# A query's V in one load of 64 keys a partition, between the two loads of the next query's K

## The chip, the cores and the metric

The kernel runs on one core of one Trainium2 chip. The metric is the device time of one execution in microseconds, as the median of several runs; profiles come from one execution each. TensorE (PE) multiplies matrices, VectorE (DVE) and ScalarE (ACT) work elementwise, GpSimd (POOL) does little here, and SyncE (SP) issues nearly all loads; 16 DMA engines move the data.

## The reference

One decode step of a transformer block in float32, for two sequences of one token each: layer norm, attention over a cache of 8192 keys with 16 heads of 256, output projection, residual; then layer norm and a bilinear gated feed-forward layer, residual.

```python
B, Sq, D = 2, 1, 448
H, Sk, Dh = 16, 8192, 256
q = (x @ wq).reshape(B, Sq, H, Dh)            # then heads ahead of tokens
scores = jnp.einsum("bhqd,bhkd->bhqk", q, k_cache) * (Dh ** -0.5)
p = _softmax(scores, axis=-1)
o = jnp.einsum("bhqk,bhkd->bhqd", p, v_cache)
# h = x + attention(layernorm(x)) @ wo
# h2 = h + ((layernorm(h) @ w_gate) * (layernorm(h) @ w_up)) @ w_down
```

The two caches hold 2 x 16 x 8192 x 256 floats each, 268 MB; all other inputs together are some 25 MB.

## The kernel before

A pair of a head and a sequence is called a query; there are 32, and each has its own 8 MiB of K and 8 MiB of V. The keys lie on the 128 partitions, 64 to a partition. A cache load brings half a query's K or V: 4096 keys that follow each other in memory, 32 a partition, so that every partition gets one run of 32 KB. The tile goes into a ring of four slots of 32 KB a partition, which K and V share.

The main loop (lines 306 to 343) runs over n from 0 to 32. Iteration n issues on SP the loads of query n's K and of query n-1's V, by turns: K's first half, V's first half, K's second half, V's second half. After the first V comes, in some iterations, a load of output weights (`load_wo`, 448 KB, where n % 4 is 1 or 3) or of query weights (`load_wq`, 896 KB, where n % 4 is 2). A load waits on SP until its slot of the ring was read for the last time, and whatever follows on SP waits behind it.

DVE scores query n's K: per 16 keys of a partition a product (L239) and a reduction (L242), four such pairs a query, and a maximum at the end (`top`, L249). A slot of K is free after its second product. In between, after the first pair of query n, DVE, PE and ACT make the softmax of query n-1 (`softmax`), and PE then mixes its V with the weights (`mix`, L278): 32 matmuls a query of two keys a partition each, which appear as 64 instructions, 32 for each half of V. `mixed` brings the result into the output projection. Where n % 4 is 3, save in the last such iteration, PE computes the next two heads' queries (`queries`, L212 and L217) between the two halves of a mix; that is in 7 iterations. PE, DVE and ACT work in the order of the code.

In the end come the feed-forward weights: `wg_t` and `wu_t` (3136 KB each) and `wd_t` (3136 KB in three loads) go into the ring as well. PE computes g (L379, `g_ps`), then u (`u_ps`), DVE multiplies the two, and L438 is the last projection. The last V half comes in parts of 16, 8 and 8 keys (`LAST`), the first K half in two of 16 (`FIRST`).

Of the kernel before, what the change touches and what calls it, by code (L numbers as in the profile page):

```python
# [8 lines left out]
F32 = mybir.dt.float32  # L9
# [4 lines left out]
B, D, H, SK, DH, F = 2, 448, 16, 8192, 256, 1792  # L14
EPS = 1e-5
P = 128
# [3 lines left out]
JC = 32  # L20
NCH = SK // (P * JC)
NJ = SK // P

FIRST, LAST = (16, 16), (16, 8, 8)
RING = 4
WQ, WO = 3 * 2 * DH + DH, 2 * D

FG = (512, 512, 384, 384)
# [1 line left out]
NF = F // P  # L30
# [13 lines left out]
def tile_decode_block(  # L44
# [20 lines left out]
    nc = tc.nc  # L65
    ctx.enter_context(tc.manual_schedule())
    const = ctx.enter_context(tc.tile_pool(name="const", bufs=1))
    ring = ctx.enter_context(tc.tile_pool(name="ring", bufs=RING))
    wpool = ctx.enter_context(tc.tile_pool(name="wpool", bufs=2))
# [77 lines left out]
    def load_wq(hp):  # L147
        t = wpool.tile([P, WQ], F32, tag="wq", name=f"wq_{hp}")
        nc.sync.dma_start(t, wq[hp])
        return t  # L150
# [6 lines left out]
            wo_t[h // 2] = wpool.tile([P, 2, WO], F32, tag="wo", name=f"wo_{h // 2}")  # L157
        nc.sync.dma_start(wo_t[h // 2][:, h % 2, :], wo[h])

    def load_cache(src, b, h, c, name, parts=(JC,)):  # L160
        t = ring.tile([P, JC, DH], F32, tag="ring", name=f"{name}_{h}_{b}_{c}")
        n = P * JC
        keys = src[b, h, c * n : (c + 1) * n].rearrange("(p j) d -> p j d", p=P)
        at = 0
        for k in parts:
            nc.sync.dma_start(t[:, at : at + k, :], keys[:, at : at + k, :])
            at += k
        return t

    w_now = load_wq(0)  # L170

# [55 lines left out]
    NQ = H * B  # L227
# [41 lines left out]
        rl_t[i] = work.tile([P, 1], F32, tag="rl", name=f"rl_{i}")  # L269
        nc.vector.reciprocal(rl_t[i], l_t[i])  # L270

    def mix(i, vt, c):

        o, p = o_ps[i % 2], p_t[i]
        for t in range(c * JC // 2, (c + 1) * JC // 2):
            j = 2 * t - c * JC
            g = 32 * (t % 4)
            nc.tensor.matmul(  # L278
                o[g : g + 2, :], p[:, 2 * t : 2 * t + 2], vt[c][:, j : j + 2, :],
                start=(t < 4), stop=(t >= NJ // 2 - 4),  # L280
            )

    def mixed(i):
# [14 lines left out]
        if b == B - 1:  # L298
            w = wo_t[h // 2][:, h % 2, :]
            for c in range(2):  # L300
# [2 lines left out]
                    start=(h == 0 and c == 0), stop=(h == H - 1 and c == 1),  # L303
                )

    for n in range(NQ + 1):
        kt, vt = [], []
        hp, at = divmod(n, 2 * B)
        for c in range(NCH):
            if n < NQ:  # L310
                parts = FIRST if n == 0 and c == 0 else (JC,)
                kt.append(load_cache(k_cache, n % B, n // B, c, "k", parts))
            if n > 0:
                parts = LAST if n == NQ and c == NCH - 1 else (JC,)
                vt.append(load_cache(v_cache, (n - 1) % B, (n - 1) // B, c, "v", parts))
            if c == 0 and at == 1:
                load_wo(2 * hp)
            if c == 0 and at == 3 and hp + 1 < H // 2:
                load_wo(2 * hp + 1)
            if c == 0 and at == 2 and hp + 1 < H // 2:  # L320
                w_t[hp + 1] = load_wq(hp + 1)
        if n == NQ:
            load_wo(H - 1)
        if n < NQ:
            scores(n, kt, 0)
        if n > 0:
            softmax(n - 1)
        if n < NQ:
            scores(n, kt, 1)
        if n > 0:  # L330
            norm(n - 1)
        if n < NQ:
            for part in range(2, 2 * NCH):
                scores(n, kt, part)
        for c in range(NCH):
            if c > 0 and at == 3 and hp + 1 < H // 2:
                q_t[hp + 1] = queries(hp + 1, w_t[hp + 1])
            if n > 0:
                mix(n - 1, vt, c)
        if n > 0:  # L340
            mixed(n - 1)
        if n < NQ:
            top(n)
# [7 lines left out]
    wg_t = load_ff(wg, "wg_t")  # L351
    wu_t = load_ff(wu, "wu_t")

    wd_t = ring.tile([P, NF, D], F32, tag="ring", name="wd_t")
    at = 0
    for n in (8, 4, 2):
        nc.sync.dma_start(
# [145 lines left out]
```

## Time and profile before

| | |
|---|---|
| median of 3 runs | 1314.98 us (1314.97 to 1315.05) |
| the profiled execution | 1314.9 us |
| its span in the trace | 1313.1 us |
| busy: DVE, PE, ACT | 1153.3, 569.9, 60.7 us |
| moved by DMA | 561.64 MB, mean 428 GB/s |

The span is the time in which instructions and transfers are recorded; the execution is 1.8 us longer. Busy times are sums over the span and say nothing yet of what waits for what; the chain that ended last does, and so do the bracketed parts of timeline rows, which give an instruction's idle time before it and what ended that.

### The profile page before, as it was taken

How to read it: one execution, taken by the hardware profiler on the slowest of the kernel's cores; microseconds unless marked ns; L12 is line 12 of the kernel's file. 1: busy time of each engine (PE TensorE's matmuls, PEld its weight loads, DVE VectorE, ACT ScalarE, POOL GpSimd, SP SyncE). 2: the span in 40 equal slices, each digit the busy share in tenths (PEclk: the TensorE clock that was granted, in tenths of full speed). 3: DMA queues.
4: the chain of work that ended last, by engine and by line, in shares of the span. 5: the costliest groups of instructions: out<-in, count | busy, mean ns of one | idle time of the engine just before them, and what ended most of it. 6: DMA issues, size and time to landing. Idle time of an engine off the chain costs nothing.

```text
span 1313.1 us, 6974 instructions
## 1 busy us (share of the span) xinstructions
PE 569.9 (43%) x2936; PEld 173.4 (13%) x2936; DVE 1153.3 (88%) x395; ACT 60.7 (5%) x183; POOL 1.2 (0%) x8
## 2 busy tenths in 40 slices
PE   3224553354432743426433453524525246254357
PEld 2011110111010210102110021101101002011013
DVE  7999999898998899888998889988998989989971
ACT  1000000000000000000000000000000000000000
POOL 0000000000000000000000000000000000000000
PEclk8556766657765666657666567666676667565668
DMA  9999999999999999999999999999999999999997
GB/s 408 430 430 433 430 432 429 428 433 433 431 428 434 430 431 426 435 429 432 431 431 431 434 429 431 430 425 434 430 431 431 433 428 435 431 430 431 431 424 336
DMA packets 23091, 561.64 MB, mean 428 GB/s; under 512 B 2578, under 2 KB 2580, under 8 KB 5908
## 3 DMA queue, kind: packets, MB, share of 16 engines
q1 hardware_dynamic: 23048, 561.20, 99.6%
q8 instruction: 23, 0.38, 0.1%
q14 instruction: 8, 0.07, 0.0%
q10 hardware_dynamic: 12, 0.01, 0.0%
HBM read 561.19 MB, written 0.00 MB: 427 GB/s over the span
## 4 chain that ended last, share of the span: by engine, by line
DMA 79%; PE 14%; DVE 5%; issue 1%; ACT 0%; POOLq 0%; SPq 0%; POOL 0%
DMA v<-in_A_v_cache_dram 77%; PE o_ps L278 13%; DVE prod L239 3%; DMA wu_t<-in_B_w_up_dram 2%; DVE s L242 2%; PE q_ps L199 0%; PE u_ps L379 0%; PE y_ps L438 0%; DVE o_ps L101 0%; PE hm_ps L431 0%; PE oT_ps L291 0%; ACT o_sb L287 0%; PE mean_x L120 0%; DVE xb L134 0%; PE var_x L178 0%
## 5 line engine op out<-in xcount | busy, mean ns | idle before, releaser
L239 DVE TENSOR_TENSOR prod<-k,q 128x4096 f32<-128x4096 f32 x128 | 565.7, 4420 | 115.6 <-DMA k<-in_A_k_cache_dram 110.7
L242 DVE TENSOR_REDUCE s<-prod 128x16 f32<-128x4096 f32 x128 | 565.8, 4420 | 6.0
L278 PE MATMUL o_ps<-v,p 128*2 128x512 f32 x2048 | 371.3, 891 | 338.1 <-DMA v<-in_A_v_cache_dram 338.1
L278 PEld LDWEIGHTS o_ps<-v,p 128*2 128x2 f32 x2048 | 59.2, 109 | 613.6 <-DMA v<-in_A_v_cache_dram 367.3
L257 PE MATMUL nb_ps<-nm,row 1*128 1x1 f32 x64 | 17.9, 347 | 280.0 <-DVE nm L255 280.0
L257 PEld LDWEIGHTS nb_ps<-nm,row 1*128 1x128 f32 x64 | 15.7, 303 | 287.2 <-issue 158.7
L287 ACT ACTIVATE o_sb<-o_ps 128x512 f32<-128x512 f32 x32 | 19.1, 597 | 679.2 <-PE o_ps L278 679.2
L301 PE MATMUL acc_ps<-wo,oT 128*2 128x448 f32 x64 | 43.9, 834 | 5.6 <-ACT oT L297 5.6
L291 PE MATMUL oT_ps<-sel,o_sb 128*128 128x1 f32 x256 | 33.7, 253 | 23.2 <-ACT o_sb L287 23.2
L212 PE MATMUL q_ps<-wq,xb 128*128 128x512 f32 x84 | 39.1, 601 | 0.0
L291 PEld LDWEIGHTS oT_ps<-sel,o_sb 128*128 128x128 f32 x256 | 31.0, 191 | 55.9 <-ACT o_sb L287 55.9
L251 PE MATMUL mT<-ident,m 128*1 128x128 f32 x32 | 10.2, 318 | 61.2 <-DVE m L249 60.9
L266 PE MATMUL l_ps<-lsum,ones 128*128 128x1 f32 x64 | 18.7, 362 | 23.5 <-ACT p L262 23.5
L259 ACT ACTIVATE nb<-nb_ps 128x1 f32<-128x1 f32 x32 | 5.5, 171 | 406.8 <-PE nb_ps L257 406.8
L266 PEld LDWEIGHTS l_ps<-lsum,ones 128*128 128x128 f32 x64 | 16.0, 310 | 26.2 <-ACT p L262 26.2
L212 PEld LDWEIGHTS q_ps<-wq,xb 128*128 128x128 f32 x84 | 15.4, 190 | 20.6 <-issue 20.3
L217 PE MATMUL q_ps<-wq,xb 128*128 128x256 f32 x56 | 14.4, 379 | 0.0
L251 PEld LDWEIGHTS mT<-ident,m 128*1 128x1 f32 x32 | 2.5, 79 | 84.7 <-issue 50.0
L389 DVE TENSOR_TENSOR h_sb<-x_sb,acc_ps 2x448 f32<-2x448 f32 x1 | 0.6, 609 | 13.8 <-PE acc_ps L301 13.8
L222 ACT ACTIVATE q<-q_ps 128x512 f32<-128x512 f32 x14 | 8.4, 597 | 92.1 <-PE q_ps L217 92.1
L217 PEld LDWEIGHTS q_ps<-wq,xb 128*128 128x128 f32 x56 | 10.6, 190 | 7.4 <-issue 6.7
L262 ACT ACTIVATE p<-s,nb 128x64 f32<-128x64 f32 x32 | 11.1, 348 | 1.0
(79 smaller groups left out, 101.8 us busy)
## 6 DMA issues: line engine op xcount, KB each, us to landing
k<-in_A_k_cache_dram SPq DMA_DIRECT2D x63, 4096.0 KB, 26.5
v<-in_A_v_cache_dram SPq DMA_DIRECT2D x63, 4096.0 KB, 33.2
wq<-in_wq_dram SPq DMA_DIRECT2D x8, 896.0 KB, 34.6
wo<-in_wo_dram SPq DMA_DIRECT2D x16, 448.0 KB, 33.5
k<-in_A_k_cache_dram SPq DMA_DIRECT2D x2, 2048.0 KB, 13.5
wg_t<-in_B_w_gate_dram SPq DMA_DIRECT2D x1, 3136.0 KB, 24.5
wu_t<-in_B_w_up_dram SPq DMA_DIRECT2D x1, 3136.0 KB, 30.4
v<-in_A_v_cache_dram SPq DMA_DIRECT2D x1, 2048.0 KB
```

The lines of the kernel that those rows point to most:

```text
L212: nc.tensor.matmul(ps, xb[:, c, b, :], w[:, c * 2 * DH : (c + 1) * 2 * DH], start=(c == 0), stop=False,)
L217: nc.tensor.matmul(ps[:, k * DH : (k + 1) * DH], xb[:, DC - 1 + k, b, :], w[:, 3 * 2 * DH : WQ], start=False, stop=(k == 1),)
L239: nc.vector.tensor_mul(prod, kt[c][:, k * HC : (k + 1) * HC, :], q[:, None, :].to_broadcast([P, HC, DH]))
L242: nc.vector.tensor_reduce(s_t[i][:, part * HC : (part + 1) * HC], prod, axis=AX.X, op=ALU.add)
L251: nc.tensor.transpose(mT_t[i], m, ident)
L257: nc.tensor.matmul(nb_ps, row, nm, start=True, stop=True)
L262: nc.scalar.activation(p_t[i], s_t[i], AF.Exp, bias=nb, scale=DH**-0.5, accum_out=lsum)
L266: nc.tensor.matmul(l_t[i], ones, lsum, start=True, stop=True)
L278: nc.tensor.matmul(o[g : g + 2, :], p[:, 2 * t : 2 * t + 2], vt[c][:, j : j + 2, :], start=(t < 4), stop=(t >= NJ // 2 - 4),)
L287: nc.scalar.activation(o_sb, o_ps[i % 2], AF.Copy)
L291: nc.tensor.matmul(oT_ps[:, c : c + 1], o_sb[:, (2 * k + c) * P : (2 * k + c + 1) * P], sel[:, k : k + 1], start=(k == 0), stop=(k == 1),)
L301: nc.tensor.matmul(acc_ps, oT_t[h][:, c, :], w[:, c * D : (c + 1) * D], start=(h == 0 and c == 0), stop=(h == H - 1 and c == 1),)
```

## The change

V of a query becomes one load of 64 keys a partition, one run of 64 KB in each, into a buffer of its own, `v_sb`, which takes 64 KB a partition; the ring keeps two slots, for K alone. K is loaded in two halves still, but a partition's 64 keys now follow each other in memory, so a half is 32 KB out of every 64. V of query n-1 is loaded between the two halves of query n's K. The first two queries' V come as 16 and 48 keys (`EARLY`), the first of these ahead of the K of the same iteration; for the second query it is issued after the first half of query 0's mix. The last query's V comes as 32, 16, 8 and 8 keys. `wd_t` moves from the ring into `v_sb`. Scores, softmax and mixing keep their instructions; only the keys' order over partitions differs, for K and V alike.

```diff
--- before.py
+++ after.py
@@ -21,8 +21,10 @@
 NCH = SK // (P * JC)
 NJ = SK // P
 
-FIRST, LAST = (16, 16), (16, 8, 8)
-RING = 4
+FIRST = (16, 16)
+
+EARLY, LAST = (16, 48), (32, 16, 8, 8)
+RING = 2
 WQ, WO = 3 * 2 * DH + DH, 2 * D
 
 FG = (512, 512, 384, 384)
@@ -157,15 +159,20 @@
             wo_t[h // 2] = wpool.tile([P, 2, WO], F32, tag="wo", name=f"wo_{h // 2}")
         nc.sync.dma_start(wo_t[h // 2][:, h % 2, :], wo[h])
 
-    def load_cache(src, b, h, c, name, parts=(JC,)):
-        t = ring.tile([P, JC, DH], F32, tag="ring", name=f"{name}_{h}_{b}_{c}")
-        n = P * JC
-        keys = src[b, h, c * n : (c + 1) * n].rearrange("(p j) d -> p j d", p=P)
+    def load_k(b, h, c, parts=(JC,)):
+        t = ring.tile([P, JC, DH], F32, tag="ring", name=f"k_{h}_{b}_{c}")
+        keys = k_cache[b, h].rearrange("(p j) d -> p j d", p=P)
         at = 0
         for k in parts:
-            nc.sync.dma_start(t[:, at : at + k, :], keys[:, at : at + k, :])
+            nc.sync.dma_start(t[:, at : at + k, :], keys[:, c * JC + at : c * JC + at + k, :])
             at += k
         return t
+
+    v_sb = const.tile([P, NJ, DH], F32, name="v_sb")
+
+    def load_v(b, h, at, to):
+        keys = v_cache[b, h].rearrange("(p j) d -> p j d", p=P)
+        nc.sync.dma_start(v_sb[:, at:to, :], keys[:, at:to, :])
 
     w_now = load_wq(0)
 
@@ -269,14 +276,13 @@
         rl_t[i] = work.tile([P, 1], F32, tag="rl", name=f"rl_{i}")
         nc.vector.reciprocal(rl_t[i], l_t[i])
 
-    def mix(i, vt, c):
+    def mix(i, c):
 
         o, p = o_ps[i % 2], p_t[i]
         for t in range(c * JC // 2, (c + 1) * JC // 2):
-            j = 2 * t - c * JC
             g = 32 * (t % 4)
             nc.tensor.matmul(
-                o[g : g + 2, :], p[:, 2 * t : 2 * t + 2], vt[c][:, j : j + 2, :],
+                o[g : g + 2, :], p[:, 2 * t : 2 * t + 2], v_sb[:, 2 * t : 2 * t + 2, :],
                 start=(t < 4), stop=(t >= NJ // 2 - 4),
             )
 
@@ -303,16 +309,26 @@
                     start=(h == 0 and c == 0), stop=(h == H - 1 and c == 1),
                 )
 
+    def loads_v(n):
+
+        parts = EARLY if n <= 2 else LAST if n == NQ else (NJ,)
+        return [((n - 1) % B, (n - 1) // B, sum(parts[:k]), sum(parts[: k + 1])) for k in range(len(parts))]
+
     for n in range(NQ + 1):
-        kt, vt = [], []
+        kt = []
         hp, at = divmod(n, 2 * B)
+        todo = loads_v(n) if n > 0 else []
+        if n == 1:
+
+            load_v(*todo.pop(0))
+        if n == 2:
+            todo.pop(0)
         for c in range(NCH):
             if n < NQ:
-                parts = FIRST if n == 0 and c == 0 else (JC,)
-                kt.append(load_cache(k_cache, n % B, n // B, c, "k", parts))
-            if n > 0:
-                parts = LAST if n == NQ and c == NCH - 1 else (JC,)
-                vt.append(load_cache(v_cache, (n - 1) % B, (n - 1) // B, c, "v", parts))
+                kt.append(load_k(n % B, n // B, c, FIRST if n == 0 and c == 0 else (JC,)))
+            if c == 0:
+                for v in todo:
+                    load_v(*v)
             if c == 0 and at == 1:
                 load_wo(2 * hp)
             if c == 0 and at == 3 and hp + 1 < H // 2:
@@ -336,7 +352,9 @@
             if c > 0 and at == 3 and hp + 1 < H // 2:
                 q_t[hp + 1] = queries(hp + 1, w_t[hp + 1])
             if n > 0:
-                mix(n - 1, vt, c)
+                mix(n - 1, c)
+                if n == 1 and c == 0:
+                    load_v(*loads_v(2)[0])
         if n > 0:
             mixed(n - 1)
         if n < NQ:
@@ -351,7 +369,7 @@
     wg_t = load_ff(wg, "wg_t")
     wu_t = load_ff(wu, "wu_t")
 
-    wd_t = ring.tile([P, NF, D], F32, tag="ring", name="wd_t")
+    wd_t = v_sb.rearrange("p j d -> p (j d)")[:, : NF * D].rearrange("p (n d) -> p n d", d=D)
     at = 0
     for n in (8, 4, 2):
         nc.sync.dma_start(
```

SP's queue in mid-kernel, before: a k or v row is half a query's K or V, named by sequence, half and a running number (`k_1_0_666`: sequence 1, first half); `wq` and `wo` are weights; at the end of a row stand partitions x floats.

```order
L166 DMA k_0_1_594<-in_A_k_cache_dram 128x8192
L166 DMA v_1_1_596<-in_A_v_cache_dram 128x8192
L166 DMA k_1_0_666<-in_A_k_cache_dram 128x8192
L166 DMA v_0_0_668<-in_A_v_cache_dram 128x8192
L158 DMA wo_515<-in_wo_dram 128x896
L166 DMA k_1_1_671<-in_A_k_cache_dram 128x8192
L166 DMA v_0_1_673<-in_A_v_cache_dram 128x8192
L166 DMA k_0_0_758<-in_A_k_cache_dram 128x8192
L166 DMA v_1_0_760<-in_A_v_cache_dram 128x8192
```

K and V take turns here, half by half. The same place after:

```order
L167 DMA k_0_1_581<-in_A_k_cache_dram 128x8192
L167 DMA k_1_0_651<-in_A_k_cache_dram 128x8192
L175 DMA v_sb<-in_A_v_cache_dram 128x16384
L160 DMA wo_505<-in_wo_dram 128x896
L167 DMA k_1_1_655<-in_A_k_cache_dram 128x8192
L167 DMA k_0_0_740<-in_A_k_cache_dram 128x8192
L175 DMA v_sb<-in_A_v_cache_dram 128x16384
L167 DMA k_0_1_743<-in_A_k_cache_dram 128x8192
```

V's two rows of 8192 floats a partition became one of 16384, and the two halves of K around a query's change now follow each other.

SP's queue at the end, before, from the last query's K to the feed-forward weights:

```order
L166 DMA k_1_0_2602<-in_A_k_cache_dram 128x8192
L166 DMA v_0_0_2604<-in_A_v_cache_dram 128x8192
L166 DMA k_1_1_2606<-in_A_k_cache_dram 128x8192
L166 DMA v_0_1_2608<-in_A_v_cache_dram 128x8192
L166 DMA v_1_0_2677<-in_A_v_cache_dram 128x8192
L166 DMA v_1_1_2679<-in_A_v_cache_dram 128x4096
L166 DMA v_1_1_2679<-in_A_v_cache_dram 128x2048 x2
L158 DMA wo_2453<-in_wo_dram 128x896
L348 DMA wg_t<-in_B_w_gate_dram 128x6272
L348 DMA wu_t<-in_B_w_up_dram 128x6272
```

The last K's second half has half a query's V between it and the first. And after:

```order
L167 DMA k_1_0_2515<-in_A_k_cache_dram 128x8192
L175 DMA v_sb<-in_A_v_cache_dram 128x16384
L167 DMA k_1_1_2518<-in_A_k_cache_dram 128x8192
L175 DMA v_sb<-in_A_v_cache_dram 128x8192
L175 DMA v_sb<-in_A_v_cache_dram 128x4096
L175 DMA v_sb<-in_A_v_cache_dram 128x2048 x2
L160 DMA wo_2371<-in_wo_dram 128x896
L366 DMA wg_t<-in_B_w_gate_dram 128x6272
L366 DMA wu_t<-in_B_w_up_dram 128x6272
L375 DMA v_sb<-in_wd_dram 128x3584
```

The second half of the last K now stands behind the whole V of the query before it, and the last V, in four parts, behind that.

## Rows read from the trace of the kernel before

**Rows 1.** The page, parts 1 and 3: busy per engine; queue, packets, MB, share

```profile
PE 569.9 (43%) x2936; PEld 173.4 (13%) x2936; DVE 1153.3 (88%) x395; ACT 60.7 (5%) x183; POOL 1.2 (0%) x8
...
q1 hardware_dynamic: 23048, 561.20, 99.6%
```

**Rows 2.** The page, part 4: the chain that ended last, by engine

```profile
DMA 79%; PE 14%; DVE 5%; issue 1%; ACT 0%; POOLq 0%; SPq 0%; POOL 0%
```

**Rows 3.** Timeline, DVE, 557 to 639: start us, us, engine, line, op, out<-in, idle before

```profile
557.05 4.42 DVE L239 TENSOR_TENSOR prod<-k,q 128x4096 f32<-128x4096 f32 x1 [2.74 <-DMA k<-in_A_k_cache_dram]
...
578.74 4.42 DVE L239 TENSOR_TENSOR prod<-k,q 128x4096 f32<-128x4096 f32 x1 [3.69 <-DMA k<-in_A_k_cache_dram]
...
598.10 4.43 DVE L239 TENSOR_TENSOR prod<-k,q 128x4096 f32<-128x4096 f32 x1 [1.32 <-DMA k<-in_A_k_cache_dram]
...
618.72 4.43 DVE L239 TENSOR_TENSOR prod<-k,q 128x4096 f32<-128x4096 f32 x1 [2.63 <-DMA k<-in_A_k_cache_dram]
...
636.55 0.22 DVE L249 TENSOR_REDUCE m<-s 128x1 f32<-128x64 f32 x1
...
638.15 4.42 DVE L239 TENSOR_TENSOR prod<-k,q 128x4096 f32<-128x4096 f32 x1 [1.38 <-DMA k<-in_A_k_cache_dram]
```

**Rows 4.** Timeline, PE: two places in mid-kernel, then the first query's mix

```profile
609.12 6.02 PE L278 MATMUL o_ps<-v,p 128*2 128x512 f32 x32
...
615.07 2.84 PE L212 MATMUL q_ps<-wq,xb 128*128 128x512 f32 x6
...
621.18 1.03 PE L217 MATMUL q_ps<-wq,xb 128*128 128x256 f32 x4
...
649.16 6.47 PE L278 MATMUL o_ps<-v,p 128*2 128x512 f32 x32
...
58.24 4.99 PE L278 MATMUL o_ps<-v,p 128*2 128x512 f32 x32
...
64.86 3.62 PE L278 MATMUL o_ps<-v,p 128*2 128x512 f32 x32 [1.64 <-DMA v<-in_A_v_cache_dram]
```

**Rows 5.** Timeline, SP's queue: a K load is issued

```profile
611.59 0.33 SPq L166 DMA_DIRECT2D k<-in_A_k_cache_dram  x1
```

**Rows 6.** Timeline, the start: x's load, its first use, the fifth cache load

```profile
0.74 0.55 ACTq L78 DMA_DIRECT2D x_sb<-in_A_x_dram  x1
...
2.26 0.45 PE L141 MATMUL T_ps_x<-ident,x_sb 2*128 2x2 f32 x3 [2.26 <-DMA x_sb<-in_A_x_dram]
...
24.87 0.33 SPq L166 DMA_DIRECT2D k<-in_A_k_cache_dram  x1
```

**Rows 7.** The page, part 2: GB/s in 40 equal slices of 32.8 us

```profile
GB/s 408 430 430 433 430 432 429 428 433 433 431 428 434 430 431 426 435 429 432 431 431 431 434 429 431 430 425 434 430 431 431 433 428 435 431 430 431 431 424 336
```

**Rows 8.** Timeline, the end, 1256 to 1307: DVE, PE and ACT

```profile
1256.39 4.42 DVE L239 TENSOR_TENSOR prod<-k,q 128x4096 f32<-128x4096 f32 x1 [1.50 <-DMA k<-in_A_k_cache_dram]
...
1274.22 0.22 DVE L249 TENSOR_REDUCE m<-s 128x1 f32<-128x64 f32 x1
...
1276.83 7.54 PE L278 MATMUL o_ps<-v,p 128*2 128x512 f32 x56
...
1285.73 1.04 PE L278 MATMUL o_ps<-v,p 128*2 128x512 f32 x8 [1.36 <-DMA v<-in_A_v_cache_dram]
...
1294.40 1.92 PE L379 MATMUL g_ps<-wg_t,xr 128*32 128x512 f32 x8 [0.68 <-DMA wg_t<-in_B_w_gate_dram]
...
1301.25 0.69 ACT L416 ACTIVATE g_sb<-g_ps,rv 128x512 f32<-128x512 f32 x1 [12.41 <-PE g_ps L379]
...
1301.77 3.65 PE L379 MATMUL u_ps<-wu_t,xr 128*32 128x256 f32 x64 [0.60 <-DMA wu_t<-in_B_w_up_dram]
...
1306.75 3.12 PE L438 MATMUL y_ps<-wd_t,hmT 128*2 128x112 f32 x112
```

## The prediction

> **What bounds the kernel now.** I read the page's first part and its queue table, then the chain, then the stretches of DVE, PE and SP around one query, then the last 60 us. [rows 1]: the one busy queue fills the 16 DMA engines for 99.6% of the span; DVE is next with 88%, 1153.3 us, that is 36.0 us for each of the 32 queries. [rows 2]: 79% of the chain is DMA, and what is left is mostly PE. [rows 3]: DVE starts each K tile just when it lands; from 598.10 to 638.15 a query takes 40.05 us, so DVE has about 4 us to spare and PE much more. So in the body only two things count: how fast bytes move, and whether the queue ever runs dry. At the end a chain of compute follows the last loads, and there order counts.
>
> **What the change does to bytes and loads.** Every byte is still loaded once. SP issues 29 cache loads fewer (161 rows become 132): the V of queries 2 to 30 is one load in place of two; the others keep their count. Price of a load: in [rows 3] V and K, 8192 KB, take 638.15 - 618.72 = 19.43 us. With a wo load (448 KB) between them they take 618.72 - 598.10 = 20.62, with a wq load (896 KB) 578.74 - 557.05 = 21.69. At the rate of the 19.43 the two would cost 1.06 and 2.13; they cost 1.19 and 2.26. Both exceed by 0.13 us, whatever their size: about the fixed price of a load of 128 runs. If a 64 KB run costs as much overhead as a 32 KB one, the change saves 29 x 0.13 = 3.8 us; if the gain of longer runs is nothing and a load itself is free, 0. No row shows a 64 KB run, or parts the load's price from that of its runs, so I take the middle, -2 us, and keep 0 and -4. The Trainium skill, "DMA: Bandwidth & Descriptors", section "Where 436 GB/s comes from", puts a ceiling of 435.2 GB/s on the engines' ports; the trace agrees that little is left, with 8192 KB in 19.43 us, 431.7 GB/s. By that page even perfect runs would save an estimated 0.16 us of each V's 19.43, 4.5 us in 29.
>
> K is now read as 32 KB out of every 64 KB. Its runs keep their length and number: 0, unless the pitch matters (a rival).
>
> **Whether the queue runs dry in the body.** Let A be the time when K's second half of query n lands and DVE starts on it. DVE takes 17.83 us to its last reduction (618.72 to 636.55, [rows 3]) and some 18 in all, so it starts K's first half of n+1 at A+18.0; that landed at A+9.7. Landings then follow at 9.72 us a 4096 KB: V(n) at A+29.15, K's second half of n+1 at A+40.05 where a wo lies between, K's first half of n+2 at A+49.8.
> - The slot of K. The ring has two slots; a slot comes free at the second product, 611.59 - 598.10 = 13.5 us after DVE began ([rows 3, 5]). So K's first half of n+2 can be issued at A+31.5 and must be on its way by about A+38.5: a tiny load takes 1.5 us from issue to use (0.74 to 2.26, [rows 6]). 7 us to spare, cost 0. K's second half has more.
> - The V buffer. V(n+1) waits on SP until PE has mixed the whole of V(n), and behind it on SP stand a wo or wq and K's second half of n+2, which DVE awaits. The weights of query n are ready 609.12 - 598.10 = 11.0 us after DVE began on the next K ([rows 3, 4]), at A+29.0, so mixing starts with V's landing, A+29.15. It is 64 instructions. Cold, 32 take 6.0 to 6.5 us; when PE has just been at work, 3.62 ([rows 4]). So a mix takes about 9.7 us and ends at A+38.9. V(n+1) must be issued by A+49.8 - 1.5 = A+48.3. Spare: 9 us.
> - In every fourth iteration, but not the last, 7 in all, the queries of the next head pair stand on PE between the two halves of a mix: 615.07 to 622.21, 7.1 us ([rows 4]). Then the mix ends at A+46.0: still 2 us to spare, cost 0. This is the cover that is thin. If both halves run at 6.47, it ends at A+49.2 and the queue stands still for 1.0 us, seven times.
> - The start. The second query's first 16 keys of V wait for the first mix, which starts at 58.24 and takes 4.99 for a half ([rows 4]), so they go out between 61 and 63.3. Ahead of them stand 26.5 MB, which at the 408 and 430 GB/s of the first slices ([rows 7]) last to 63.4. K's first half of query 1 goes out at 24.87, when DVE frees the first slot ([rows 6]: there it was the fifth cache load), with 11.4 MB ahead of it, to 28. Cost 0, at worst 1.4.
>
> **The end, where the change costs.** Before, the order is K0(31), V0(30), K1(31), V1(30), V0(31), V1(31) in three parts. Now the whole V(30) stands ahead of K1(31). That puts K1(31) 4096 KB later, half of 19.43: it lands not at 1256.39 but at 1266.11 ([rows 8]). All that DVE and PE do with it follows:
> - last reduction of DVE after 1274.22 - 1256.39 = 17.83: 1283.94;
> - first instruction of the last mix after 1276.83 - 1274.22 = 2.61: 1286.55.
> The last part of V(31) has the same bytes ahead of it as before, so it lands when it did, 1285.73, and no longer decides. Before, 56 of the 64 instructions were done while the last parts of V were under way, and 1.04 us was left after the landing: end at 1286.77. Now all 64 come after the softmax: PE has been idle before, so 6.0 + 3.62 = 9.7 us, end at 1296.25, 9.5 us later. Bounds: 7.2 warm (end 1293.8, +7.0) and 12.9 all cold (1299.5, +12.7).
> What hides of this: before, the first down-stream projection started at 1294.40 as its weights landed and ended at 1301.2, and the next one then waited 0.60 us for the wu load ([rows 8]). That 0.6 is absorbed. So u starts at 1301.2 + 9.5 = 1310.7 in place of 1301.77: **+8.9 us**, bounds +6.4 and +12.1. After u nothing waits for a load: wd's 3136 KB follow wu and land by about 1309, while their user, at 1306.75 before ([rows 8]), would start near 1315.7. wd now goes into the V buffer and waits for the first 13 matmuls of the last mix, about 1290, when wg is still moving: 0.
>
> **Sum.** The profiled execution took 1314.9 us (span 1313.1 and 1.8 around it), 0.1 below the median. 1314.9 + 8.9 - 2.0 + 0 = **1321.8**. Its own range: 1314.9 + 6.4 - 4 = 1317.3 to 1314.9 + 12.1 = 1327.
>
> **Rivals.**
> 1. The V buffer stalls the queue: the seven query iterations at cold pace, 7 x 1.0 = 7 us, 1328.8. For it: the 2 us of spare rest on PE running fast after its first half, and the mix at 649.16 stayed at 6.47 through all of its 32 ([rows 4]). Against: the 3.62 and the queries' 7.1 behind a mix of 6.02 show PE fast when it works on. It decides from a mix with queries longer than 19.1 us. 12%.
> 2. The pitch slows the reads: V and K now step 64 KB from partition to partition. If they moved at the pace of the body's slowest slices, 425 GB/s in place of 431 ([rows 7]), the 64 pairs of loads of 19.43 us would grow by 1.4%, 17 us: 1339. Against: wu with its 24.5 KB runs lands 1301.77 - 1294.40 = 7.4 us after wg ([rows 8]), 3136 KB at some 435 GB/s, hardly other than the 32 KB runs, so the step shows no hold so far. 8%. The Trainium skill, "DMA: Bandwidth & Descriptors", section "Latency and other measured facts", tells of lower rates at large power-of-two row pitches, from 512 KiB up; it gives no figure for 64 KB, and no run here shows one.
> 3. Long runs pay for the end: not slower. The engines would have to save 0.3 us of each V's 19.43 to cover the 8.9, twice the 0.13 that the rows bear out, and 0.4 us to be faster: 64 KB runs at 440 GB/s: 29 x 0.4 = 11.6 us, 1312. Only if a run itself costs much more than the excess of wo and wq shows. 12%, half of it faster.
>
> **How the numbers follow.** Forecast 68%, rivals 12, 8 and 12. A change of 0.2%, 2.6 us, is about the least that a measurement of this kernel tells from none. The forecast's low end touches the upper edge of that band (1317.6), 3% of the cases. So faster 0.06, same 0.09, slower 0.85. Range: from the forecast's low end 1317 to 1329, which takes in rival 1 and leaves out rivals 2 and 3, 20%.
>
> **What would show it.** In the profile after: DVE's last K tile starts near 1264 to 1266; the last mix is one block of 64 instructions that starts some 2.6 us after DVE's last reduction and not after a landing; u starts after g and not after wu's landing; the chain's last 50 us are DVE and PE. The DMA share stays at 99% in every slice of the body; one V and two halves of K take about 38.7 us. The prediction is wrong if DVE waits for K longer than some 4 to 6 us in any query (rival 1), if GB/s fall evenly (rival 2) or rise above 435 (rival 3).

## The result

The changed kernel takes 1320.59 us (median of 6 runs, 1318.19 to 1322.65), the kernel before 1314.97 (1314.78 to 1315.05): a ratio of 1.0040, 95% interval 1.0029 to 1.0051. Forecast were 1321.8 us in a range of 1317 to 1329, that is 1.0052, and slower. The profiled execution took 1322.65 us with a span of 1320.8; it is the slowest of the six. New is the scatter: 4.5 us between runs, where the kernel before has 0.3 in this comparison and 1.0 to 2.4, with more runs, in those of the experiments below.

A version found on the way (`e9_best`, below) takes 1313.17 us, 0.9984 of the kernel before (0.9976 to 0.9993).

### The profile page after: what moved, and what is told of

The parts are those of the page before. It is cut to its first block, busy times and chain, and to the rows that moved or that the text cites. A ratio compares the mean times of both kernels' runs of the same rounds, so it can differ in the third digit from the quotient of the medians.

```text
span 1320.8 us, 6916 instructions
## 1 busy us (share of the span) xinstructions
PE 494.1 (37%) x2936; PEld 167.7 (13%) x2936; DVE 1150.8 (87%) x395; ACT 60.7 (5%) x183; POOL 1.2 (0%) x8
## 3 DMA queue, kind: packets, MB, share of 16 engines
q1 hardware_dynamic: 18872, 561.19, 98.9%
## 4 chain that ended last, share of the span: by engine, by line
DMA 62%; DVE 34%; PE 3%; issue 0%; ACT 0%; DVEq 0%; POOLq 0%; POOL 0%
DMA k<-in_A_k_cache_dram 62%; DVE prod L246 22%; DVE s L249 12%; PE o_ps L284 1%; PE g_ps L397 0%; PE q_ps L206 0%; PE u_ps L397 0%; PE y_ps L456 0%; PE acc_ps L307 0%; PE oT_ps L297 0%; DVE o_ps L103 0%; PE hm_ps L449 0%; DVEq L246 0%; DVE h_sb L407 0%; ACT o_sb L293 0%
## 5 line engine op out<-in xcount | busy, mean ns | idle before, releaser
L284 PE MATMUL o_ps<-v_sb,p 128*2 128x512 f32 x2048 | 301.2, 751 | 0.6 <-DMA v_sb<-in_A_v_cache_dram 0.4
L284 PEld LDWEIGHTS o_ps<-v_sb,p 128*2 128x2 f32 x2048 | 54.2, 98 | 214.2 <-issue 211.9
L307 PE MATMUL acc_ps<-wo,oT 128*2 128x448 f32 x64 | 36.2, 701 | 5.6 <-ACT oT L303 5.6
L293 ACT ACTIVATE o_sb<-o_ps 128x512 f32<-128x512 f32 x32 | 19.1, 597 | 271.7 <-PE o_ps L284 271.7
## 6 DMA issues: line engine op xcount, KB each, us to landing
k<-in_A_k_cache_dram SPq DMA_DIRECT2D x63, 4096.0 KB, 19.7
```

The costliest lines, as they stand in the source:

```text
L284: nc.tensor.matmul(o[g : g + 2, :], p[:, 2 * t : 2 * t + 2], v_sb[:, 2 * t : 2 * t + 2, :], start=(t < 4), stop=(t >= NJ // 2 - 4),)
L293: nc.scalar.activation(o_sb, o_ps[i % 2], AF.Copy)
L307: nc.tensor.matmul(acc_ps, oT_t[h][:, c, :], w[:, c * D : (c + 1) * D], start=(h == 0 and c == 0), stop=(h == H - 1 and c == 1),)
```

## The profile after

The page of the changed kernel, parts 1 to 4: busy time, GB/s in 40 slices, the queue, and the chain that ended last. They answer to [rows 1], [rows 7] and [rows 2].

```profile
PE 494.1 (37%) x2936; PEld 167.7 (13%) x2936; DVE 1150.8 (87%) x395; ACT 60.7 (5%) x183; POOL 1.2 (0%) x8
...
GB/s 404 415 439 432 431 437 425 431 431 438 433 429 425 431 431 437 429 427 430 435 432 431 435 425 427 428 448 425 427 422 433 428 442 429 437 421 433 433 422 243
...
q1 hardware_dynamic: 18872, 561.19, 98.9%
...
DMA 62%; DVE 34%; PE 3%; issue 0%; ACT 0%; DVEq 0%; POOLq 0%; POOL 0%
```

DVE's work is what it was; PE's busy time fell from 569.9 to 494.1 us, nearly all of it in the mixes (371.3 to 301.2 us), which now run on in one block. The queue is busy for 98.9% of a longer span, before for 99.6% of a shorter one. The two places where GB/s fell are the second slice, 415 in place of 430, and the last, 243 in place of 336: in between they scatter round the same 431. The chain has 34% of DVE where there were 5%. That share is not of the end: in every query the chain now takes 13.3 us of DVE, from a landing to the second product, which frees a slot for K, and then the K load that waited for the slot. A piece of the chain just ahead of the end (start us, us, what):

```profile
1239.51 25.31 DMA k<-in_A_k_cache_dram
```

For some 15 of these 25 us the load stands behind V in the queue (9.72 us are its own). It lands at 1264.8, and what follows, 55.9 us or 4% of the span, is DVE and PE, with short pieces of ACT and no load.

Now the body, the same iteration as in [rows 4], a timeline of PE, DVE and SP (start us, us, engine, line, op, out<-in, idle before):

```profile
616.80 6.40 PE L284 MATMUL o_ps<-v_sb,p 128*2 128x512 f32 x32
...
623.13 2.84 PE L219 MATMUL q_ps<-wq,xb 128*128 128x512 f32 x6
...
628.13 4.43 DVE L246 TENSOR_TENSOR prod<-k,q 128x4096 f32<-128x4096 f32 x1 [4.44 <-DMA k<-in_A_k_cache_dram]
...
630.20 3.62 PE L284 MATMUL o_ps<-v_sb,p 128*2 128x512 f32 x32
...
633.88 0.33 SPq L175 DMA_DIRECT2D v_sb<-in_A_v_cache_dram  x1
...
667.26 4.43 DVE L246 TENSOR_TENSOR prod<-k,q 128x4096 f32<-128x4096 f32 x1 [3.25 <-DMA k<-in_A_k_cache_dram]
```

DVE waits once a query, 4.44 and 3.25 us, when the second half of K lands; the first half it takes without waiting. A whole cycle from landing to landing is 39.13 us here. Three more such landings, two early and one late in the body, are used further below:

```profile
107.52 4.42 DVE L246 TENSOR_TENSOR prod<-k,q 128x4096 f32<-128x4096 f32 x1 [6.09 <-DMA k<-in_A_k_cache_dram]
...
148.00 4.43 DVE L246 TENSOR_TENSOR prod<-k,q 128x4096 f32<-128x4096 f32 x1 [4.53 <-DMA k<-in_A_k_cache_dram]
...
1108.69 4.43 DVE L246 TENSOR_TENSOR prod<-k,q 128x4096 f32<-128x4096 f32 x1 [4.26 <-DMA k<-in_A_k_cache_dram]
```

The mix with the queries in it takes from 616.80 to 633.82, 17.0 us, and the V load goes out right behind, 633.88.

The end, which answers to [rows 8]:

```profile
1264.91 4.43 DVE L246 TENSOR_TENSOR prod<-k,q 128x4096 f32<-128x4096 f32 x1 [2.82 <-DMA k<-in_A_k_cache_dram]
...
1282.74 0.22 DVE L256 TENSOR_REDUCE m<-s 128x1 f32<-128x64 f32 x1
...
1285.65 9.92 PE L284 MATMUL o_ps<-v_sb,p 128*2 128x512 f32 x64
...
1303.37 1.92 PE L397 MATMUL g_ps<-wg_t,xr 128*32 128x512 f32 x8 [0.50 <-DVE xr L136]
...
1309.29 4.04 PE L397 MATMUL u_ps<-wu_t,xr 128*32 128x256 f32 x62
...
1309.96 0.69 ACT L434 ACTIVATE g_sb<-g_ps,rv 128x512 f32<-128x512 f32 x1 [12.32 <-PE g_ps L397]
...
1314.66 2.87 PE L456 MATMUL y_ps<-v_sb,hmT 128*2 128x112 f32 x112
```

The last reduction of DVE comes at 1282.74 (1274.22 before), the last mix is one block of 64 instructions of 9.92 us that starts 2.91 us later, and u (the row at 1309.29, where g's last two instructions overlap) follows g and waits for no load; the last projection starts at 1314.66, 7.9 us later than before. The chain from DVE's last tile at 1264.91 to the end of the span takes 55.9 us.

## The experiments

Times are medians; each ratio is against the kernel before in the same session, which took 1315.03 to 1315.13. A ratio goes by all runs, so where the runs scatter it is not quite the quotient of the two medians.

### The order at the end, by itself, in the kernel before: e2_late_k

```diff
-            if n < NQ:
+            late = n == NQ - 1 and c == NCH - 1
+            if n < NQ and not late:
                 ...
                 kt.append(load_cache(k_cache, ...))
             if n > 0:
                 vt.append(load_cache(v_cache, ...))
+            if late:
+                kt.append(load_cache(k_cache, ...))
```

> The kernel before with one thing changed: the second half of the last K is issued behind the second half of the V of the query before it. Nothing else of the change is in it: ring of four, 32 KB runs. Theory (order at the end alone makes the loss): DVE starts the last K tile 9.7 us later, at 1266, the last mix starts at 1286.5 as one block of 9 to 10 us, and the time rises by 7.7 to 9: 1322.7 to 1324. Rival (body): 1315.0, no change.

Measured: 1323.54 us (1319.74 to 1324.13), ratio 1.0058 (1.0046 to 1.0070), 8.5 us above the kernel before. Its timeline at the end:

```profile
1266.08 4.43 DVE L239 TENSOR_TENSOR prod<-k,q 128x4096 f32<-128x4096 f32 x1 [11.22 <-DMA k<-in_A_k_cache_dram]
...
1283.91 0.22 DVE L249 TENSOR_REDUCE m<-s 128x1 f32<-128x64 f32 x1
...
1286.82 9.96 PE L278 MATMUL o_ps<-v,p 128*2 128x512 f32 x64
```

The tile lands at 1266.08 (forecast 1266.11), the mix starts at 1286.82 (1286.55) and takes 9.96 us. Two loads that change places in an otherwise untouched kernel make a loss as large as the whole change's 5.6 us, and larger. And the scatter comes with it.

### The end put back in the changed kernel: e1_tail, e6_tail2, e11_tail4

`e1_tail` splits the V of the last query but one and puts the last K's second half between; `e6_tail2` and `e11_tail4` have `n >= NQ - 2` and `n >= NQ - 4` in its place.

```diff
-        parts = EARLY if n <= 2 else LAST if n == NQ else (NJ,)
+        parts = EARLY if n <= 2 else LAST if n == NQ else (JC, JC) if n == NQ - 1 else (NJ,)
...
             if c == 0:
+                late = [todo.pop()] if n == NQ - 1 else []
                 for v in todo:
                     load_v(*v)
+            else:
+                for v in late:
+                    load_v(*v)
```

> The changed kernel with one thing put back: the V of the last query but one comes in two loads of 32 keys, and the second half of the last K stands between them, where it stood in the kernel before. Theory (the loss is the last K that lands one half load later, so that the last mix comes whole after the last softmax): DVE starts the last K tile near 1255, the last mix is split by the landing of the last V part, u waits for wu again, and the loss of some 8 us is gone: 1312 to 1315, with the runs close together again, since the end hangs on transfers and not on a chain of compute. Rival (the body moves slower, by pitch or by stalls): stays at 1319 to 1321.

Measured: 1317.27 us (1315.63 to 1322.25), ratio 1.0024 (1.0014 to 1.0033). Less came back than expected, and the scatter stayed. Its timeline shows why:

```profile
1227.59 4.43 DVE L246 TENSOR_TENSOR prod<-k,q 128x4096 f32<-128x4096 f32 x1 [3.78 <-DMA k<-in_A_k_cache_dram]
...
1245.55 4.42 DVE L246 TENSOR_TENSOR prod<-k,q 128x4096 f32<-128x4096 f32 x1
...
1263.49 4.42 DVE L246 TENSOR_TENSOR prod<-k,q 128x4096 f32<-128x4096 f32 x1
...
1284.23 8.86 PE L284 MATMUL o_ps<-v_sb,p 128*2 128x512 f32 x64
...
1299.58 1.05 PE L401 MATMUL g_ps<-wg_t,xr 128*32 128x512 f32 x8 [0.50 <-DVE xr L136]
...
1303.92 0.69 ACT L438 ACTIVATE g_sb<-g_ps,rv 128x512 f32<-128x512 f32 x1 [8.75 <-PE g_ps L401]
```

DVE starts the last tile at 1263.49 and without a wait: the tile had landed. From 1227.59 on, where DVE last waited, it works without a pause, three halves of K, 18 us each. So it is not the landing of the last tile alone that is late; all K halves stand closer together since the change, second half and next first half in a row, and DVE has 54 us of work in front of it when the last second half but one lands. The changed kernel's own row says the same: of the 8.5 us by which its last tile starts later than before (1264.91 against 1256.39), the wait for the landing is only 2.82; without it DVE would have started at 1262.1.

> As e1_tail, but the V of the last three queries is split, so that the last two queries' K halves both stand between halves of V. e1_tail moved the last K tile's landing back, but DVE had not yet worked off the K tiles before it, which the new order brings close together: it started on the last tile near 1264 all the same. Theory (it is the time at which DVE is done with the last K that counts, and the scatter of the runs is that of a chain of compute at a changing PE clock): DVE starts the last tile at 1256 to 1257, u waits for wu, 1314.5 to 1316, and the runs within 1 us of each other. Rival (the body loses as much and scatters): 1317 with a scatter of 5 us, as e1_tail.

Measured: 1316.27 us (1314.61 to 1317.97), ratio 1.0009 (1.0000 to 1.0018). DVE starts the last tile at 1260.59 there: one more query in the old order gives it 2.9 us, no more, about the wait that DVE has in a query without weights, 2.82 us at the changed kernel's last tile: more than that it can't work off in one. This missed the 1256 that were expected.

> The changed kernel with its order at the end alone put back further: the V of the last five queries in halves, by turns with the K halves, so that DVE has four queries in which to work off what lands together. Queries and start as in the change. Theory (the whole end is back, what is left is the body): DVE is done with the last K at 1274 to 1275.5 as before the change, u waits for wu, runs within 1 us, 1315 to 1316.3: the change's body by itself is 0 to 1.3 us slower than before (64 KB runs -2, late V loads +2, start +1). Rival (the body scatters too): runs still spread over 3 us or more.

Measured: 1315.16 us (1313.98 to 1317.05), ratio 1.0001 (0.9992 to 1.0010). Its end:

```profile
1256.67 4.42 DVE L246 TENSOR_TENSOR prod<-k,q 128x4096 f32<-128x4096 f32 x1 [1.50 <-DMA k<-in_A_k_cache_dram]
...
1274.50 0.22 DVE L256 TENSOR_REDUCE m<-s 128x1 f32<-128x64 f32 x1
...
1285.93 1.04 PE L284 MATMUL o_ps<-v_sb,p 128*2 128x512 f32 x8 [1.15 <-DMA v_sb<-in_A_v_cache_dram]
...
1301.94 0.69 ACT L438 ACTIVATE g_sb<-g_ps,rv 128x512 f32<-128x512 f32 x1 [12.90 <-PE g_ps L401]
...
1301.97 3.65 PE L401 MATMUL u_ps<-wu_t,xr 128*32 128x256 f32 x64
```

DVE starts the last tile at its landing, 1256.67, and is done at 1274.50; one last piece of the mix follows the landing of V at 1285.93, as before the change, and u follows g by 0.03 us, so that the end stands just at the balance of loads and compute. With the end put back, 5.4 us of the changed kernel's 5.6 are gone, and its body alone costs nothing that can be measured (four of its V, though, come in halves here). Some 3 us of scatter are left, and the kernel before has 1.6 in the same session, so a part was not of the end: the rival of `e11_tail4` was right there.

### PE's clock in the chain at the end: e10_warm

```diff
+        if n == NQ - 1:
+            warm = ps_q.tile([P, 2 * P], F32, tag="q", name="warm")
+            for _ in range(24):
+                nc.tensor.matmul(warm, ident, xb[:, 0].rearrange("p b r -> p (b r)"), start=True, stop=True)
         if n < NQ:
             top(n)
```

First two rows of a view: the stretch from 1300 to 1305 of the changed kernel and then of `e1_tail` (busy us and count of PE, PEld, DVE, ACT, POOL, then PE's granted clock, DMA share, GB/s).

```profile
1300.00:1305.00 5.00, 3.54 (x23) 1.31 (x22) 2.57 (x13) 0.00 (x0) 0.00 (x0) 0.50 0.97 410
```

```profile
1300.00:1305.00 5.00, 4.85 (x64) 2.35 (x60) 1.04 (x6) 0.69 (x1) 0.00 (x0) 1.00 0.96 408
```

Both kernels run g in or near this stretch, the one with a granted clock of 0.50, 1.2 GHz, the other with 1.00, 2.4 GHz. From g's first instruction to the ACT instruction behind it `e1_tail` takes 1303.92 - 1299.58 = 4.3 us, the changed kernel 1309.96 - 1303.37 = 6.6; the mixes take 8.86 and 9.92. So the same instructions differ by 3.3 us with the level of the clock. With the short instructions between mix and g, from the mix's start to that ACT instruction, it is 19.7 us in `e1_tail` and 24.3 in the changed kernel, 4.6 more; from DVE's start on the last tile to the mix's start both take 20.74. Ahead of g there is the same row of short PE instructions in both; why the clock fell in the one and not in the other, the rows don't show.

> The changed kernel with 24 matmuls added whose result nobody reads, on PE while it waits for DVE's last K tile (between 1267 and about 1283). Nothing else is changed. Theory (the end is a chain of compute whose length hangs on PE's clock): PE is at the faster level when the last mix starts, the mix takes 7 to 8 us in place of 9.9, and the time falls by 2 to 3 us to 1317.5 to 1319. Rival (the end hangs on transfers, or the clock has fallen again by then): no change, 1320.6, or later if the added work stands in the way.

Measured: 1321.92 us (1319.57 to 1323.95), ratio 1.0045 (1.0032 to 1.0059): no gain in total, against the theory's number. Two places of its profiled execution (span 1321.6):

```profile
789.83 4.43 DVE L246 TENSOR_TENSOR prod<-k,q 128x4096 f32<-128x4096 f32 x1 [3.95 <-DMA k<-in_A_k_cache_dram]
...
795.73 0.33 SPq L175 DMA_DIRECT2D v_sb<-in_A_v_cache_dram  x1
...
830.16 4.43 DVE L246 TENSOR_TENSOR prod<-k,q 128x4096 f32<-128x4096 f32 x1 [4.45 <-DMA k<-in_A_k_cache_dram]
...
1269.21 4.42 DVE L246 TENSOR_TENSOR prod<-k,q 128x4096 f32<-128x4096 f32 x1 [2.83 <-DMA k<-in_A_k_cache_dram]
...
1270.99 10.61 PE L363 MATMUL warm<-xb,ident 128*128 128x256 f32 x48
...
1289.94 8.32 PE L284 MATMUL o_ps<-v_sb,p 128*2 128x512 f32 x64
```

The mix takes 8.32 us, less than 9.92 and more than 7 to 8: the added work ends at 1281.6, and between 1285 and 1290 the granted clock is 0.57. From the last tile's start to the end of the span it is 52.4 us in place of 55.9, so the chain did get shorter by 3.5. But the last tile landed at 1269.21, 4.3 us later than in the profile of the changed kernel, though all that is added lies behind it. That loss lies ahead of the added work, and the first three rows show a part of it: next section. With five and six runs that scatter by more than 4 us, the 1.3 between the two medians is no difference. What the clock is worth in the total is therefore not settled by this run; that the chain's length hangs on it is.

### The V load behind the queries: e5_queries, e7_tail2_queries, e12_later

```diff
         for c in range(NCH):
-            if c > 0 and at == 3 and hp + 1 < H // 2:
-                q_t[hp + 1] = queries(hp + 1, w_t[hp + 1])
             if n > 0:
                 mix(n - 1, c)
         if n > 0:
             mixed(n - 1)
+        if at == 2 and hp + 1 < H // 2:
+            q_t[hp + 1] = queries(hp + 1, w_t[hp + 1])
```

> As e1_tail, but the queries of the next head pair are computed one iteration earlier, after the mix and ahead of the maximum's transposition, and no longer between the halves of a mix, so that a mix takes 9 to 10 us in every iteration and the V buffer is free 7 us earlier in seven of them. Theory A (the cover of 2 us holds): as e1_tail within 0.5 us. Theory B (the V load is late there by some tenths of a us each time): 1 to 2.5 us below e1_tail.

Measured, on `e1_tail`: 1315.64 us (1315.18 to 1320.18), ratio 1.0014 (1.0005 to 1.0022), 1.6 us below `e1_tail`; the runs of the two, and their intervals, overlap.

> As e6_tail2, with the queries one iteration earlier as in e5_queries. Theory (seven late V loads cost some 2 us in all, and 64 KB runs save 2.2): 1312.5 to 1314, so 1.5 to 2.5 us below e6_tail2 and below the kernel before. Rival (no late loads): as e6_tail2.

Measured, on `e6_tail2`: 1314.81 us (1313.55 to 1316.70), ratio 0.9997 (0.9988 to 1.0005), 1.5 us below `e6_tail2`, and not clear of the kernel before. Twice some 1.5 us: the cover that the prediction called thin was not there. The medians alone would not carry that; the cycles show it. One without weights in it takes 666.59 - 627.81 = 38.78 us in `e9_best`, which has the queries early (rows below); its V load went out at 625.91, 11.6 us before the K half ahead of it landed (627.81 + 9.72 = 637.5). In the changed kernel it goes out at 633.88, 4.0 us before that landing at 637.85, and the cycle is 39.13, 0.35 more; over the seven such cycles, with loads 3.4 to 5.2 us ahead, it is between nothing and 0.4, 1.7 in all. In `e10_warm` it goes out at 795.73, 3.8 us before, and the cycle is 830.16 - 789.83 = 40.33, 1.55 more. (The landing ahead is an estimate: 9.72 us, half of the 19.43 of the prediction, behind DVE's start.) The same cycles are above 38.78 by 1.6 to 2.4 us in all in `e1_tail`, `e6_tail2` and `e11_tail4` and by 6.0 in `e10_warm`, but by 0.0 to 0.4 in the three kernels with the queries early.

The other cycles lose something too, whatever the V loads do. In `e9_best` two cycles with a wo load exceed the usual 39.9 by 1.5 and 1.7 us, 480 us apart (546.94 - 505.51 = 41.43 is the first), with V loads 9.6 and 10.8 us ahead; the kernel before has two such losses, 1.4 and 1.5 us, 481 apart (20.78 us at 536.27 and 20.82 at 1017.37 in place of 19.36). What makes them is not shown, and the 1.55 of `e10_warm` may be one. So the whole stretch is the better measure. Over 24 cycles, from the K that lands near 148 to the one that lands near 1109, the changed kernel takes 1108.69 - 148.00 = 960.7 us and `e9_best` 1108.01 - 147.59 = 960.4; `e5_queries` and `e7_tail2_queries` take 960.3 and 960.5, and with late loads `e11_tail4` takes 961.5, `e1_tail` 961.7, `e6_tail2` 961.8 and `e10_warm` 962.7. The late loads cost 0.3 us in the profile of the changed kernel and 1.0 to 2.5 in the others.

> As e9_best, with the queries back between the halves of a mix and, behind them, 8 matmuls of 0.44 us whose result nobody reads, in the same seven iterations. The V load there goes out 3.5 us later than in the changed kernel, about 0.4 us before the K tile ahead of it has landed. Theory A (a load must go out 1.5 us ahead of that landing, as the prediction took it): the queue stands for 1.1 us seven times, 8 us: 1321. Theory B (it must go out some 5.5 us ahead, as the losses of 0.1 to 1.5 us with loads 3.7 to 6 us ahead suggest): 5 us seven times, 35 us: 1348.

```diff
+                more = ps_q.tile([P, 2 * P], F32, tag="q", name=f"more_{hp}")
+                for _ in range(8):
+                    nc.tensor.matmul(more, ident, xb[:, 0].rearrange("p b r -> p (b r)"), start=True, stop=True)
```

Measured: 1330.26 us (1328.59 to 1331.90), ratio 1.0112 (1.0095 to 1.0129), 17.1 us above `e9_best`. In the trace six of the seven cycles have a late load and lose 16.6 in all; in the seventh V comes in halves. One of them:

```profile
636.09 4.42 DVE L246 TENSOR_TENSOR prod<-k,q 128x4096 f32<-128x4096 f32 x1 [3.98 <-DMA k<-in_A_k_cache_dram]
...
645.26 0.33 SPq L175 DMA_DIRECT2D v_sb<-in_A_v_cache_dram  x1
...
676.99 4.42 DVE L246 TENSOR_TENSOR prod<-k,q 128x4096 f32<-128x4096 f32 x1 [5.02 <-DMA k<-in_A_k_cache_dram]
```

The load goes out at 645.26, 0.55 us before the landing at 636.09 + 9.72 = 645.81, and the cycle takes 40.90, 2.1 us more than 38.78. By that a load must be out some 2.7 us before the landing of the one ahead, in others of the six up to 4.0. Neither theory's number is met: 1.5 us is too little, 5.5 is more than the full stop needs. That loads 3.4 to 5 us ahead lose nothing in some cycles and up to 1.5 in others is not explained by it; the cause stays open.

### Run length and pitch: e4_two_loads, e8_two_loads, e3_pitch

```diff
-(JC, JC) if n >= NQ - 2 else (NJ,)
+(JC, JC)
```

This is the edit of `e8_two_loads`; in `e4_two_loads` the condition that goes is `n == NQ - 1`.

> As e1_tail, but every query's V comes in two loads of 32 keys that follow each other, into the same buffer, so that all runs are 32 KB again. Theory (a 64 KB run in place of two of 32 KB saves some 0.07 us of a V): 2 us above e1_tail. First rival (the price of 0.13 us of a load of 128 runs, as for wo and wq): 3.5 us above. Second rival (run length is worth nothing): as e1_tail.

Measured, on `e1_tail`: 1318.80 us (1316.61 to 1321.57), ratio 1.0027 (1.0018 to 1.0036), 1.5 us above, with runs that scatter by 5.0 and 6.6. This one doesn't tell the theories apart: with V in two loads, the first waits only for the first half of the mix, so the late loads go as well as the long runs.

> As e7_tail2_queries, with every V but the first two and the last in two loads of 32 keys a partition that follow each other. Theory (64 KB runs save 0.075 us of a V): 2 us above e7_tail2_queries. Rivals: 3.5 us above (price of a load as for wo and wq), or none.

Measured, on `e7_tail2_queries`, where no load is late: 1316.00 us (1314.98 to 1319.31), ratio 1.0008 (0.9999 to 1.0017), 1.2 us above. The scatter of the two makes that a poor measure; the landings are a better one. `e8_two_loads`, DVE's starts on the second half of K over a cycle without weights:

```profile
628.73 4.43 DVE L246 TENSOR_TENSOR prod<-k,q 128x4096 f32<-128x4096 f32 x1 [4.05 <-DMA k<-in_A_k_cache_dram]
...
667.57 4.42 DVE L246 TENSOR_TENSOR prod<-k,q 128x4096 f32<-128x4096 f32 x1 [2.90 <-DMA k<-in_A_k_cache_dram]
```

38.84 us, and 38.78 in `e9_best`. All such cycles agree, 38.84 to 38.86 in the one and 38.77 to 38.79 in the other: one load with 64 KB runs in place of two with 32 KB saves 0.06 to 0.07 us of a V, 1.9 us in 29. The theory, not the 0.13 that wo and wq suggested; what of it is the run and what the second load, no run parts.

```diff
-        n = P * JC
-        keys = src[b, h, c * n : (c + 1) * n].rearrange("(p j) d -> p j d", p=P)
+        keys = src[b, h].rearrange("(p j) d -> p j d", p=P)[:, c * JC : (c + 1) * JC, :]
```

> The kernel before with the keys laid out over the partitions as in the change (64 keys that follow each other on a partition), still in halves: all runs are 32 KB and step 64 KB from partition to partition, for K and V. Order, ring and loads as before. Theory (the step costs nothing): 1315.0 within 0.5 us. Rival (the step slows the reads to the pace of the slowest slices, 425 GB/s): up to 1332.

Measured: 1315.05 us (1314.93 to 1315.84), ratio 0.9998 (0.9989 to 1.0007). A step of 64 KB with runs of 32 costs nothing; rival 2 falls.

### All of it together: e9_best

`e11_tail4` with the queries early, and with

```diff
-        parts = EARLY if n <= 2 else LAST if n == NQ else ...
+        parts = EARLY if n == 1 else LAST if n == NQ else ...
-        if n == 2:
-            todo.pop(0)
...
-                if n == 1 and c == 0:
-                    load_v(*loads_v(2)[0])
```

> As e11_tail4, with the queries one iteration earlier, and with the second query's V whole behind its K and no longer in 16 and 48 keys. Theory (each part by itself: late loads 2 us, start 0.6 of its 1.0 us, 64 KB runs kept): 1312.5 to 1313.7, faster than the kernel before by 1.3 to 2.5 us, runs within 1 us. Rival (the gain of the runs is taken by something later): 1314.5 to 1315.5.

Measured: 1313.17 us (1313.00 to 1313.75), ratio 0.9984 (0.9976 to 0.9993): 1.9 us faster than the kernel before and 7.4 faster than the changed one, and the scatter is down to 0.75 us, where the kernel before has 1.6 in the same session. Its body and its u:

```profile
107.68 4.42 DVE L246 TENSOR_TENSOR prod<-k,q 128x4096 f32<-128x4096 f32 x1 [5.96 <-DMA k<-in_A_k_cache_dram]
...
147.59 4.42 DVE L246 TENSOR_TENSOR prod<-k,q 128x4096 f32<-128x4096 f32 x1 [3.96 <-DMA k<-in_A_k_cache_dram]
...
505.51 4.42 DVE L246 TENSOR_TENSOR prod<-k,q 128x4096 f32<-128x4096 f32 x1 [2.84 <-DMA k<-in_A_k_cache_dram]
...
546.94 4.43 DVE L246 TENSOR_TENSOR prod<-k,q 128x4096 f32<-128x4096 f32 x1 [5.49 <-DMA k<-in_A_k_cache_dram]
...
625.91 0.33 SPq L175 DMA_DIRECT2D v_sb<-in_A_v_cache_dram  x1
...
627.81 4.42 DVE L246 TENSOR_TENSOR prod<-k,q 128x4096 f32<-128x4096 f32 x1 [3.96 <-DMA k<-in_A_k_cache_dram]
...
666.59 4.43 DVE L246 TENSOR_TENSOR prod<-k,q 128x4096 f32<-128x4096 f32 x1 [2.84 <-DMA k<-in_A_k_cache_dram]
...
1108.01 4.43 DVE L246 TENSOR_TENSOR prod<-k,q 128x4096 f32<-128x4096 f32 x1 [3.96 <-DMA k<-in_A_k_cache_dram]
...
1300.10 3.65 PE L397 MATMUL u_ps<-wu_t,xr 128*32 128x256 f32 x64 [1.71 <-DMA wu_t<-in_B_w_up_dram]
```

u waits again, 1.71 us, for wu: the chain of compute has been taken off the end, and PE's clock with it. The other order at the start gains nothing that the landings show: the second half of the third query's K lands at 107.68 here and at 107.52 in the changed kernel, and the next query's at 147.59, against 147.46 to 147.49 in `e1_tail`, `e5_queries` and `e6_tail2`, which have the changed kernel's start (148.00 in the changed kernel itself, whose cycle ahead of it loses 0.6). The part of the expectation that counted on the start was wrong.

## Why the prediction was right, and where it was not

- **The order at the end** was the main term and carried the forecast. By its steps: last tile 1266.11 forecast, 1264.91 in the changed kernel and 1266.08 in `e2_late_k`; last reduction 1283.94, then 1282.74 and 1283.91; mix start 1286.55, then 1285.65 and 1286.82; mix 9.7, then 9.92 and 9.96. The 8.9 us stand against 8.8 between the spans of `e2_late_k` (1322.0) and of the kernel before in the same session (1313.2). In the changed kernel the median shows less, 5.4 us between it and `e11_tail4`. Its six runs lie 3.2 to 7.7 above the kernel before; the one with a profile is the slowest of them, and in that g ran at a granted clock of 0.50. What the faster runs did was not seen; that 4.6 us of the chain hang on the clock is what `e1_tail`'s end shows. So the term was right for a chain at the lower clock and too large for the median: the bounds of 6.4 to 12.1 looked at the mix's clock and left out g's.
- **The cause of it** was put too narrowly. The forecast let one tile land late. In truth DVE's whole queue of work is bunched, and putting that one tile's load back gave 3 us, not 8, and moved DVE's start on it by 1.4; with two queries in the old order it started at 1260.59, with four at its landing, 1256.67.
- **64 KB runs**: -2.0 forecast, a gain of 1.9 measured on the landings. The ceiling of 435.2 GB/s that the Trainium skill gives ("DMA: Bandwidth & Descriptors", section "Where 436 GB/s comes from") agrees: 16 MiB in 38.78 us are 432.6 GB/s, in the 38.84 of `e8_two_loads` 432.0.
- **The V buffer** was the failed step. "Must be issued by A+48.3" counted 1.5 us from a tiny load in an idle queue. In `e12_later` the full queue needed 2.7 to 4.0 us, and loads 3.4 to 5 us ahead lost up to 0.4 in the changed kernel and more in others. The mix's own times were right: 17.0 us with queries against 16.8, V issued at A+5.8 of the next cycle (633.88 - 628.13) against A+6. The 0 should have been 0.3 to 2.5 us by the traces, some 1.5 by the medians. Nor could the signs of rival 1 show it: the mix is shorter than its 19.1 us, and waits of DVE of 5.49 and 5.96 us stand in `e9_best`, where no V is late.
- **The start** was put at 0, at worst 1.4, and the 0 holds: the second slice's 415 GB/s are not seen in the landings, which come as early at 107.52 as with the other start of `e9_best`, 107.68. It was not tried by itself.
- So two errors of opposite sign meet. The end's term was larger than the median's by 3.5, and the body, forecast 2.0 below the kernel before, came out even with it (`e11_tail4`), with the late loads as the part of that which is shown. That 1321.8 comes so near to 1320.6 is in part luck.
- **Rival 2** (pitch) fell to `e3_pitch`. The Trainium skill, "DMA: Bandwidth & Descriptors", section "Latency and other measured facts", tells, for copies between HBM tensors, of lower rates at pitches from 512 KiB up; 64 KB, read into SBUF, has no loss here. **Rival 1** was right in kind, a late V load in the iterations with queries, but not in its cause, a slow mix, nor in its size of 7 us. **Rival 3** fell: the runs bring 0.07 us a V where 0.3 were needed.
- What the forecast said nothing of is the scatter. The kernels whose end hangs on transfers and that have no late load spread least (0.9 us in `e3_pitch`, 0.75 in `e9_best`, 0.3 to 2.4 in the kernel before); those whose end is a chain on PE, or with a load in the body late by a hair, spread by 3.1 to 6.6. That the one makes the other is likely and not shown.

## What to carry to other kernels

In a kernel that is bound by transfers, look at the order of the last loads by the work that each still needs: a load that needs 20 us of work behind it must not move back by one place, even where the sum of bytes and the busy queue stay the same, and putting it back helps in full only once the engine that works on it has no backlog. A single buffer that is reloaded while others' loads run needs its last reader done several us before the load ahead lands, by a measured lead under load and not by the latency of a small transfer. Longer runs alone, from 32 to 64 KB, were worth 0.15% here.

## What the runs showed that was not expected

- In a full queue the time by which a load must be issued before the one ahead lands is 2.7 to 4.0 us (`e12_later`: in its six late cycles the load went out 0.0 to 1.6 us ahead, and 1.2 to 3.8 were lost), against 1.5 us from issue to use of a small load in an empty one.
- Runs of one kernel, 1318.19 to 1322.65 us, scatter by 4.5 us where PE stands on the path at the end; with the end put back and the queries early the scatter is 0.75 us in `e9_best`.
- A loss of some 1.5 us comes twice in the body, about 480 us apart, in the kernel before as in `e9_best`, in cycles where no load is late. Its cause stays open; whoever reads a single cycle must know of it.
